# The first batch runs its sixteen feed-forward tiles in a row; the second batch is prepared like the later ones

## The chip, the cores and the metric

The kernel runs on one core of one Trainium2 chip. The metric is device time in microseconds, from launch to end. The profile describes one execution of it; its span runs from the first to the last instruction on the core.

## The reference

Two stages, in float32. The weights `moe_w_in` and `moe_w_out` arrive as 8-byte floats, which the kernel has to turn into 4-byte ones itself.

```python
B, H, S, Ns, D = (8, 8, 512, 32, 64)
scores  = scale * x @ state^T        ; a  = softmax(scores)  ; xread = a  @ state
scores2 = scale * state @ x^T        ; a2 = softmax(scores2) ; sread = a2 @ x
attn = concat([xread, sread], axis=2)               # per head: 512 + 32 rows of 64
x = attn.transpose(0, 2, 1, 3).reshape(8 * 544, 512)
h = x @ w_in                                        # 512 -> 2048
g = h * clip(h + 3, 0, 6) / 6
out = g @ w_out                                     # 2048 -> 512
```

## The kernel before

**Tiling.** The 2048 feed-forward columns are 16 tiles of 128, in 4 chunks of 4. A batch (512 tokens) meets the 16 tiles one by one; tile and batch together are a *step*, numbered n. Of a step, `first(n)` makes h for 512 tokens (6 matmuls 128x512: each factor is held as a high and a low part, and a product is three matmuls), ScalarE (ACT) and VectorE (DVE) make g from it and split it (`g_hi`, `g_lo`), and `second(n)` multiplies by one tile of `w_out` into the four accumulators `acc0` to `acc3` (12 matmuls), two steps later (`LAG`). Tile 0 of batch 0 is computed "plain", in float32 without the split. Step numbers 128 to 143 are the rows of `sread` of all batches together.

**W'.** `xread @ w_in` is not formed: `wprime` multiplies the batch's state with a chunk of `w_in` (lines L507, in `all_heads`), and `first` multiplies the softmax weights (`aT_hi`, `aT_lo`) with that product (`wp_hi`, `wp_lo`).

**Preparing a batch.** Scores, softmax over the states, softmax over the tokens, and `sread`. Batches from `TURNED` on are loaded in 32x32 blocks, so that DVE transposes alone turn x and state (`load_turned`, `load_state`: 16 loads of x into `raw` buffers; `attention`). Earlier batches are loaded plainly and turned by TensorE (PE) against an identity (`take_in`, lines L591 and L620, copied out by L624); their scores use `apart`, the state with heads set apart by zeros (`all_heads_apart`, L520). Batch 0 has a variant of its own (`tokens_by_rows`, L685 to L719). Before the change `TURNED` is 2. Batch 1's x is loaded into an output buffer `ot`, turned, and loaded again into `xb` later for `sread`.

**Weights.** 16 tiles each of `w_in` and `w_out` are fetched by the SP queue, in pairs (1 MB) into four staging buffers `early0` to `early3` or singly (0.5 MB) into the three `raw` buffers. A tile is decoded by ACT (L372, `tops`) and DVE (L377, join); a `w_out` tile is then split by ACT (L403) and DVE (L405). A staging buffer takes its next pair only when the one before is decoded (for `w_out`: split). `PLACES` says which pair goes where.

**Order.** Every operation is told to a planner (`Plan`) with a cost, a rank and its inputs; `Plan.order` lists them, and each engine runs its share in that order. The first operations are listed outright, by number, in the table `OPENING`; behind its end ranks decide. Where the plan has PE idle ahead of the first step, `issue` puts dummy matmuls (`wake`).

**Sequence of steps.** Weights arrive while steps run, so before the change the first two batches share them: tiles 0 to 3 of batch 0, 0 to 7 of batch 1, 4 to 15 of batch 0, 8 to 15 of batch 1. Each of the two batches then ends in two parts, added together in `ot`:

```python
segments = [(0, 0, 1), (1, 0, 2), (0, 1, NCH), (1, 2, NCH)]
segments += [(b, 0, NCH) for b in range(2, B + 1)]
```

Of the kernel before, what the change touches and what calls it, by code (L numbers as in the profile page):

```python
# [59 lines left out]
class Plan:  # L60
# [6 lines left out]
    WARM = 7.5  # L67
# [132 lines left out]
def tile_state_attention_then_hardswish_ffn(  # L200
# [82 lines left out]
    def Q(rank, size, do, reads=(), writes=(), after=()):  # L283
        return plan.add("Q", 0.45, rank, do, reads, writes, after, size)
# [131 lines left out]
    TURNED = 2  # L416
# [30 lines left out]
    def x_key(b):  # L447
        return ("ot", "x1") if b == 1 else ("xb", b)

    def read_key(b):  # L450
        return ("xb", b)

    def x_tile(b, read=False):

        if b == 1 and not read:
            t = get(x_key(b), lambda: outp.tile([P, J, DO], F32, name="ot")).rearrange("p j e -> p (j e)")
        else:
            t = get(read_key(b), lambda: att.tile([P, J, H, D], F32, name="xb", bufs=1))  # L460
            if b >= TURNED:
                return t.rearrange("p j h d -> p h j d")
            t = t.rearrange("p j h d -> p (j h d)")
        return t.rearrange("p (h j d) -> p h j d", h=H, j=J)

    def x_parts(b, read=False):
        key = read_key(b) if read else x_key(b)
# [44 lines left out]
    def all_heads_apart(b, out):  # L512
# [3 lines left out]
        for u in range(NG):  # L516
            for q in range(NQ):
                for i in range(2):
                    rows, cols = slice(i * D, (i + 1) * D), slice(u * S // 2, (u + 1) * S // 2)
                    nc.tensor.matmul(  # L520
                        out[i][q * NS : (q + 1) * NS, cols], apart[rows, b, q, u, i], xT(b, q)[rows, cols],
# [54 lines left out]
    def xT_key(b, q):  # L576
        return (("w_out_hi1", "w_in3")[b], "xT", q) if b < 2 else ("tmp", ("xT", b, q))

    def xT(b, q):

        if b == 0:
            return get(xT_key(0, q), lambda: cpool.tile(
                [P, NQ, S], F32, name="xT", tag="w_out_hi1"))[:, q]
        return w_in_of(3, "xT")[:, q] if b == 1 else tmp(xT_key(b, q))

    def take_in(b, rank, after=(), banks=None):
# [13 lines left out]
        for u in range(NG) if b < TURNED else ():  # L600
            for i in range(2):
                def put(u=u, i=i):
                    src = bank(st)[u * D : (u + 1) * D, :P].rearrange("p (q n) -> p q n", n=NS)
# [1 line left out]
                    copy(apart[i * D : (i + 1) * D, b, :, u, i], src)
# [279 lines left out]
    def put(c, ps, cols):  # L885
# [3 lines left out]
            [n for k, n in scores_at.items() if k in (0, ("L", 0), ("L", 1), ("C", 1))])  # L889

    def tokens_read(b, tag="ps_s"):
# [11 lines left out]
        def read():  # L903
            for u in range(NG):
                for j in range(J):
                    for q in range(NQ):
# [4 lines left out]
                            x_tile(b, True)[:, NG * q + u, j, :],  # L911
# [15 lines left out]
        return 1.0 + 0.11 * len(last), read, [*t_key, *x_parts(b, True), *last_key], [pr], then, first  # L927
# [28 lines left out]
    def first(n):  # L956
# [43 lines left out]
        rank = n if b < 2 else n - 1.5  # L1000
# [91 lines left out]
    segments = [(0, 0, 1), (1, 0, 2), (0, 1, NCH), (1, 2, NCH)]  # L1092
    segments += [(b, 0, NCH) for b in range(2, B + 1)]
# [94 lines left out]
    for b, s0 in (0, 4), (1, 8):  # L1188

        def late(b=b, s0=s0):  # L1190
            rank = lambda k: LATE[b] + k * LATE_STEP[b]
            states(b, rank, scores_by_columns(b, LATE[b] + 0.01, (), "L"))
            if b == 0:
                weights_turned(b, rank(7))
            else:
                load_x(1, AGAIN, (), True)
        at(LATE_TOLD[b], late)
    at(MOVED + 1, lambda: weights_moved(1, MOVED, [first_of[MOVED]]))
    fetch(2, 28, 20)
    for b in range(2, B):  # L1200
        s0 = {2: 24}.get(b, 16 * (b - 1))
        begin(b, s0, 4 if b == 3 else 0)
        if b < B - 1:
            fetch(b + 1, s0 + 9 + (4 if b == 3 else 0), s0 + 9 + (4 if b == 3 else 0))
# [76 lines left out]
```

## Time and profile before

| | us |
|---|---|
| runs of the kernel | 652.94, 654.09, 655.06 (median 654.09) |
| the profiled execution | 654.81 |
| its span | 652.7 |
| granted TensorE clock, mean | 1.000 |

The profile gives, by engine, busy time in the span and in stretches of it; a timeline of instructions with the idle time ahead of each and what ended it; the chain of work that ended last, followed back from the end; and the DMA issues with their time to landing. PE, PEld, DVE, ACT and SP are TensorE's matmuls, its weight loads, VectorE, ScalarE and the queue of SyncE that issues DMAs.

### The profile page before, as it was taken

The page shows a single profiled execution, that of the slowest core. Times are in us where ns is not written, and L with a number is a line of the kernel's source. Part 1 is how long each engine was busy: PE and PEld are TensorE (multiplying, and loading weights), DVE is VectorE, ACT ScalarE, POOL GpSimd, SP SyncE. Part 2 cuts the span into 40 slices and gives each one's busy share as a digit, 9 for nine tenths or more (in the row PEclk, how much of TensorE's full clock was granted, in tenths as well). Part 3 has the DMA queues.
Part 4 walks back from the last instruction along what each step waited for, and adds up shares of the span by engine and source line. Part 5 has one row for each costly group of instructions (what it writes and reads, how often), then busy time and mean ns, then how long its engine had stood idle before and what let it go on. Part 6 is the DMA issues. An engine that isn't in the chain of part 4 may idle for free.

```text
span 652.7 us, 10021 instructions
## 1 busy us (share of the span) xinstructions
PE 642.7 (98%) x3991; PEld 502.7 (77%) x3991; DVE 394.8 (60%) x687; ACT 299.1 (46%) x524; POOL 1.2 (0%) x7
## 2 busy tenths in 40 slices
PE   7899999999999999999999999999999999999997
PEld 6576777777877877787868787787778787788896
DVE  5997657568747756944586356834595344443552
ACT  5778577334434343633344344534344333433542
POOL 0000000000000000000000000000000000000000
PEclk9999999999999999999999999999999999999999
DMA  8851442514253054132131405041131001000101
GB/s 255 331 178 51 150 173 90 88 26 131 32 134 65 15 82 111 25 52 46 67 66 22 76 1 134 2 69 27 66 66 31 3 1 65 1 1 1 65 1 32
DMA packets 124399, 46.25 MB, mean 71 GB/s; under 512 B 111041, under 2 KB 118721, under 8 KB 124097
## 3 DMA queue, kind: packets, MB, share of 16 engines
q1 hardware_dynamic: 124208, 45.36, 27.3%
q8 instruction: 31, 0.51, 0.3%
q10 hardware_dynamic: 144, 0.26, 0.1%
q14 instruction: 16, 0.12, 0.1%
HBM read 33.02 MB, written 8.91 MB: 64 GB/s over the span
## 4 chain that ended last, share of the span: by engine, by line
PE 94%; DMA 3%; ACT 1%; SPq 1%; DVE 1%; issue 0%
PE acc L951 56%; PE ps_h L951 29%; PE ps_s L507 4%; PE ps_h L507 2%; DMA ot<-in_x_dram 1%; DMA early<-in_moe_w_out_dram 1%; PE ps_h L908 1%; PE acc L1020 1%; DMA st_raw<-in_state_dram 0%; ACT tops L372 0%; SPq L426 0%; PE ps_h L980 0%; PE ps_s L520 0%; SPq L476 0%; DVE w_in L377 0%
## 5 line engine op out<-in xcount | busy, mean ns | idle before, releaser
L951 PE MATMUL acc<-w_out_hi,g_hi 128*128 128x512 f32 x540 | 214.1, 396 | 0.0
L951 PE MATMUL acc<-w_out_lo,g_hi 128*128 128x512 f32 x540 | 210.8, 390 | 0.0
L951 PE MATMUL acc<-w_out_hi,g_lo 128*128 128x512 f32 x540 | 210.5, 390 | 0.0
L1001 ACT ACTIVATE g<-ps_h,three 128x512 f32<-128x512 f32 (+1 forms) x144 | 95.6, 665 | 210.7 <-PE ps_h L951 210.5
L1003 DVE SCALAR_TENSOR_TENSOR g<-g,ps_h 128x512 f32<-128x512 f32 (+1 forms) x144 | 94.7, 658 | 146.0 <-ACT g L1001 144.8
L951 PEld LDWEIGHTS acc<-w_out_hi,g_hi 128*128 128x128 f32 x540 | 101.5, 188 | 34.6 <-issue 12.4
L299 DVE TENSOR_TENSOR g_lo<-g,g_hi 128x512 fp32r<-128x512 f32 (+1 forms) x143 | 94.2, 659 | 54.8 <-ACT g_hi L298 53.3
L298 ACT CAST g_hi<-g 128x512 fp32r<-128x512 f32 (+1 forms) x143 | 85.2, 596 | 84.8 <-DVE g L1003 79.3
L951 PEld LDWEIGHTS acc<-w_out_hi,g_lo 128*128 128x128 f32 x540 | 101.5, 188 | 21.4
L951 PEld LDWEIGHTS acc<-w_out_lo,g_hi 128*128 128x128 f32 x540 | 101.6, 188 | 19.8 <-issue 0.3
L951 PE MATMUL ps_h<-aT_hi,wp_hi 128*128 128x512 f32 (+1 forms) x254 | 93.0, 366 | 0.2 <-ACT wp_hi L298 0.2
L951 PE MATMUL ps_h<-aT_hi,wp_lo 128*128 128x512 f32 (+1 forms) x254 | 92.4, 364 | 0.1
L951 PE MATMUL ps_h<-aT_lo,wp_hi 128*128 128x512 f32 (+1 forms) x254 | 92.2, 363 | 0.0
L951 PEld LDWEIGHTS ps_h<-aT_hi,wp_hi 128*128 128x128 f32 x254 | 47.9, 189 | 11.2 <-issue 1.2
L951 PEld LDWEIGHTS ps_h<-aT_hi,wp_lo 128*128 128x128 f32 x254 | 47.9, 189 | 8.0 <-DVE wp_lo L299 0.5
L951 PEld LDWEIGHTS ps_h<-aT_lo,wp_hi 128*128 128x128 f32 x254 | 48.0, 189 | 7.8
L951 PE MATMUL ps_h<-aT_hi,wp 128*128 128x512 f32 x128 | 44.6, 390 | 0.0
L951 PEld LDWEIGHTS ps_h<-aT_hi,wp 128*128 128x128 f32 x128 | 24.0, 188 | 5.0
L951 PE MATMUL ps_h<-aT_lo,wp 128*128 128x512 f32 x64 | 24.9, 390 | 0.0
L299 DVE TENSOR_TENSOR wp_lo<-ps_s,wp_hi 128x512 fp32r<-128x512 f32 (+1 forms) x36 | 20.9, 608 | 5.4 <-ACT wp_hi L298 5.4
L372 ACT CAST tops<-early 128x512 f16<-128x512 bf16 x25 | 19.1, 787 | 9.7 <-DMA early<-in_moe_w_in_dram 5.0
L507 PE MATMUL ps_s<-w_in,stT 64*32 64x512 f32 (+1 forms) x352 | 22.1, 553 | 0.1
(131 smaller groups left out, 433.4 us busy)
## 6 DMA issues: line engine op xcount, KB each, us to landing
xb<-in_x_dram SPq DMA_DIRECT2D x32, 256.0 KB, 4.3
out_dram<-ot SPq DMA_DIRECT2D x8, 1024.0 KB, 4.3
early<-in_moe_w_in_dram SPq DMA_DIRECT2D x7, 1023.0 KB, 8.0
raw<-in_x_dram SPq DMA_DIRECT2D x96, 64.0 KB, 2.1
early<-in_moe_w_out_dram SPq DMA_DIRECT2D x4, 1023.5 KB, 6.0
raw<-in_moe_w_out_dram SPq DMA_DIRECT2D x7, 511.8 KB, 6.1
raw<-raw SPq DMA_DIRECT2D x96, 32.0 KB, 2.0
ot<-in_x_dram SPq DMA_DIRECT2D x4, 256.0 KB, 6.8
```

The costliest lines, as they stand in the source:

```text
L298: S_(cost, rank, lambda: nc.scalar.copy(hi(), src()), reads, [writes[0]])
L299: V(cost, rank, lambda: nc.vector.tensor_tensor(lo(), src(), hi().bitcast(F32), op=ALU.subtract), [*reads, writes[0]], [writes[1]])
L372: nc.scalar.copy(out[..., 1], digits(pieces().bitcast(BF16), 2, i))
L507: nc.tensor.matmul(out[u][cols, :], made["stT", b][rows, cols], moving(q)[rows], start=True, stop=True,)
L908: nc.tensor.matmul(bank(pr)[cols, u * D : (u + 1) * D], e2T(b, u)[:, j * P + q * NS : j * P + (q + 1) * NS], x_tile(b, True)[:, NG * q + u ...
L951: nc.tensor.matmul(ps, l, r, start=start and k == 0, stop=stop and k == n - 1)
L1001: S_(cost + 0.05, rank, lambda: nc.scalar.activation(g(), bank(ps)[:, :width], AF.Relu, bias=three), [ps], [g_key])
L1003: V(cost, rank, lambda: nc.vector.scalar_tensor_tensor(g(), g(), 6.0, bank(ps)[:, :width], op0=ALU.min, op1=ALU.mult), [ps], [g_key])
L1020: nc.tensor.matmul(bank(acc), made["g_hi", n][:, js], plain_out[i][1](), start=opens, stop=closes)
```

## The change

`TURNED` becomes 1, and the segments are the batches in their order:

```diff
-    TURNED = 2
+    TURNED = 1
...
-    segments = [(0, 0, 1), (1, 0, 2), (0, 1, NCH), (1, 2, NCH)]
-    segments += [(b, 0, NCH) for b in range(2, B + 1)]
+    segments = [(b, 0, NCH) for b in range(B + 1)]
...
-    apart = sread_t.rearrange("p q m -> p (q m)").rearrange(
-        "p (b q u i n) -> p b q u i n", b=2, q=NQ, u=NG, n=NS)
-    nc.gpsimd.memset(apart[:, 0], 0.0)
+    apart = sread_t.rearrange("p q m -> p (q m)")[:, : 2 * NG * NQ * NS].rearrange(
+        "p (q u i n) -> p q u i n", q=NQ, u=NG, n=NS)
+    nc.gpsimd.memset(apart, 0.0)
...
-        return ("ot", ("wp", b, c)) if 1 < b < B and (NCH * b + c) % 3 == 2 else ("wp", (b, c))
+        return ("ot", ("wp", b, c)) if 0 < b < B and (NCH * b + c) % 3 == 2 else ("wp", (b, c))
...
-        return (("w_out_hi1", "w_in3")[b], "xT", q) if b < 2 else ("tmp", ("xT", b, q))
+        return ("w_in3", "xT", q) if b == 0 else ("tmp", ("xT", b, q))
...
-    for b, s0 in (0, 4), (1, 8):
-
-        def late(b=b, s0=s0):
-            rank = lambda k: LATE[b] + k * LATE_STEP[b]
-            states(b, rank, scores_by_columns(b, LATE[b] + 0.01, (), "L"))
-            if b == 0:
-                weights_turned(b, rank(7))
-            else:
-                load_x(1, AGAIN, (), True)
-        at(LATE_TOLD[b], late)
-    at(MOVED + 1, lambda: weights_moved(1, MOVED, [first_of[MOVED]]))
-    fetch(2, 28, 20)
-    for b in range(2, B):
-        s0 = {2: 24}.get(b, 16 * (b - 1))
-        begin(b, s0, 4 if b == 3 else 0)
+    def late():
+        rank = lambda k: LATE[0] + k * LATE_STEP[0]
+        states(0, rank, scores_by_columns(0, LATE[0] + 0.01, (), "L"))
+        weights_turned(0, rank(7))
+    at(LATE_TOLD, late)
+    fetch(1, 4, 4)
+    for b in range(1, B):
+        s0 = {1: 6}.get(b, 16 * (b - 1))
+        begin(b, s0)
...
-    load_state(1, RANKS["st1"])
...
-    load_x(1, RANKS["x1"])
...
-        if 1 < b < B and n % (2 * FPC) == 0:
+        if 0 < b < B and n % (2 * FPC) == 0:
...
-        if n == 0:
-            take_in(1, [*RANKS["take1"], RANKS["take1"][1]], [scores_at[0]])
-            rank1 = lambda k: RANKS["soft1"][k]
-            tokens_by_columns(1, rank1, scores_by_columns(1, RANKS["scores1"], [wp_at[0, 0, 2]]))
```

So batch 1's x and state come as 32x32 blocks during batch 0's steps, its x is loaded into `xb` once (the copy in `ot` is gone), and its W' is formed for two chunks at a time. The planner's costs for DMA issues rise a little (0.45 to 0.49, 0.9 to 1.35), its `WARM` falls from 7.5 to 4.5, and the ranks of the opening are written anew. `OPENING` is a new list, of some 660 numbers where there were some 490; both begin alike:

```diff
-5 2 1 4 0 3 24 6 80 28 81 36 30 32 27 33 31 29 40 37 79 93 34 41 78 50 35 38 25 85 51 66 52 39 26 42 53 11 67
+5 2 1 0 24 3 4 35 11 80 36 27 6 29 30 28 93 31 32 33 14 49 34 41 25 19 50 51 37 26 52 42 38 39 53 43 57 54 44
```

What the list does is seen on the engines. Lines of code move down or up a little: L620 of before is L617 of the change, L716 is L713, L377 is L384, L403 is L410, L405 is L412, L363 is L370.

PE, the stretch that ends in the first step of batch 0. L620 turns the last quarter of batch 1's x, L716 turns batch 0's finished softmax weights (`ot` is the buffer of either), L507 is W' of `w_in` tiles, L980 is `first(0)`. Before:

```order
L620 MATMUL ps_s<-ident,ot 128x128 x4
L716 MATMUL acc_302<-ident,ot 128x128 x4
L716 MATMUL acc_310<-ident,ot 128x128 x4
L507 MATMUL ps_s<-w_in_190,stT 32x256 x8
L980 MATMUL ps_h<-w_in_315,tmp 128x512 x2
L507 MATMUL acc_352<-w_in_190,stT 32x128
L507 MATMUL acc_353<-w_in_190,stT 32x128
```

The same place in the change (L520 are batch 0's scores over the tokens, the `wake` rows are dummies):

```order
L520 MATMUL ps_s<-w_in_132,sread_t 32x256 x16
L1235 LDWEIGHTS wake
L1235 MATMUL ps_h<-wake 128x256
L1235 LDWEIGHTS wake
L1235 MATMUL ps_h<-wake 128x256
L1235 LDWEIGHTS wake
L1235 MATMUL ps_h<-wake 128x256
L713 MATMUL acc_302<-ident,ot 128x128 x4
L713 MATMUL acc_308<-ident,ot 128x128 x4
```

No turn of batch 1's x stands ahead of L713 any more, W' of tiles 2 and 3 stands behind `first(0)` now, and batch 0's scores over the tokens have come ahead of it.

SP's queue, the weight loads behind those of the opening. Before:

```order
L363 DMA early_342<-in_moe_w_in_dram 128x4x1023
L363 DMA early_347<-in_moe_w_out_dram 128x2047
L363 DMA early_362<-in_moe_w_in_dram 128x4x1023
L363 DMA early_365<-in_moe_w_in_dram 128x4x1023
L363 DMA early_504<-in_moe_w_out_dram 128x2x2047
L363 DMA raw<-in_moe_w_out_dram 128x2047 x2
L363 DMA early_602<-in_moe_w_out_dram 128x2x2047
```

In the change, with the same sizes:

```order
L370 DMA early_390<-in_moe_w_in_dram 128x4x1023
L370 DMA raw<-in_moe_w_out_dram 128x2047
L370 DMA early_444<-in_moe_w_out_dram 128x2x2047
L370 DMA raw<-in_moe_w_out_dram 128x2047
L370 DMA early_497<-in_moe_w_out_dram 128x2x2047
L440 DMA st_raw<-in_state_dram 32x4x32 x4
L370 DMA raw<-in_moe_w_out_dram 128x2047
L370 DMA early_562<-in_moe_w_in_dram 128x4x1023
L370 DMA early_595<-in_moe_w_in_dram 128x4x1023
L370 DMA early_641<-in_moe_w_out_dram 128x2x2047
L370 DMA early_683<-in_moe_w_out_dram 128x2x2047
L494 DMA raw<-in_x_dram 32x16x32 x16
```

The pairs 444, 562 and 641 use one staging buffer (`early2`) one after the other, and 497, 595 and 683 another (`early3`); the 16 block loads of batch 1's x stand behind them, where none stood before.

DVE in the change, where these pairs are decoded among the steps (L1000 and `g_lo` belong to steps, `wp_lo` to W', `tops` rows are joins, `w_out_lo` splits):

```order
L412 TENSOR_TENSOR w_out_lo_545<-early_497,w_out_hi_534 128x1024
L306 TENSOR_TENSOR g_lo<-g,g_hi 128x512
L384 SCALAR_TENSOR_TENSOR raw<-raw,tops 128x512
L384 SCALAR_TENSOR_TENSOR w_in_613<-early_562,tops 128x4x128
L306 TENSOR_TENSOR g_lo<-g,g_hi 128x512
L384 SCALAR_TENSOR_TENSOR w_in_613<-early_562,tops 128x4x128
L306 TENSOR_TENSOR wp_lo<-ps_s,wp_hi 128x256
L1000 SCALAR_TENSOR_TENSOR g<-g,ps_h 128x512
L384 SCALAR_TENSOR_TENSOR raw<-raw,tops 128x512
L306 TENSOR_TENSOR wp_lo<-ps_s,wp_hi 128x256
L384 SCALAR_TENSOR_TENSOR w_in_613<-early_595,tops 128x4x128 x2
```

A join that waits for its pair holds up the `g_lo` rows queued behind it.

More of the change, by code (lines that the diff above doesn't have):

```diff
@@ L24 @@
 RANKS = {
-    "load": [-0.94, -21.67, -18.89, -39.86, 11.26, 12.58, 4.72],
-    "decode": [-40.16, 63.8, 0.9, -42.8, -3.86, -8.59, -1.85], "sooner": [-6.2, 2.14, 9.66, 2.27],
-    "out_sooner": -1.74, "late": [55.57, 156.43], "late_step": [-17.01, -157.0], "halves": [47.68, -16.73],
+    "load": [-40.0, -30.0, -18.0, -28.0, -17.0, -16.0, -15.0],
+    "decode": [-40.0, -30.0, -18.0, -28.0, -17.0, -16.0, -15.0], "sooner": [0, 4.0, 4.0, 4.0],
+    "out_sooner": -1.74, "late": [4.0], "late_step": [0.3], "halves": [47.68, -16.73],
     "out_halves": [17.05, 4.87, -12.12, -22.97], "halves_first": 5.19, "again": 77.67, "moved": 22,
@@ L66 @@
     AFTER = {"T": 0.25, "V": 0.12, "S": 0.12, "Q": 0.0}
-    WARM = 7.5
+    WARM = 4.5
     def __init__(self, slots, transfer):
@@ L283, in Q @@
     def Q(rank, size, do, reads=(), writes=(), after=()):
-        return plan.add("Q", 0.45, rank, do, reads, writes, after, size)
+        return plan.add("Q", 0.49, rank, do, reads, writes, after, size)
     def get(key, make):
@@ L436, in load_state @@
         if b < TURNED:
-            plan.add("Q", 0.9, rank, load, (), [key], after, 200.0)
+            plan.add("Q", 1.35, rank, load, (), [key], after, 400.0)
             return
@@ L447, in x_key, with x_tile, x_parts, load_x @@
     def x_key(b):
-        return ("ot", "x1") if b == 1 else ("xb", b)
-    def read_key(b):
         return ("xb", b)
-    def x_tile(b, read=False):
-        if b == 1 and not read:
-            t = get(x_key(b), lambda: outp.tile([P, J, DO], F32, name="ot")).rearrange("p j e -> p (j e)")
-        else:
[L460 to L467, printed above, removed]
+    def x_tile(b):
+        t = get(x_key(b), lambda: att.tile([P, J, H, D], F32, name="xb", bufs=1))
+        if b >= TURNED:
+            return t.rearrange("p j h d -> p h j d")
+        return t.rearrange("p j h d -> p (j h d)").rearrange("p (h j d) -> p h j d", h=H, j=J)
+    def x_parts(b):
+        key = x_key(b)
         return [(*key, "q", q) for q in range(NQ)] if b < TURNED else [(*key, j) for j in range(J)]
-    def load_x(b, rank, after=(), read=False):
-        for k, key in enumerate(x_parts(b, read)):
+    def load_x(b, rank, after=()):
+        for k, key in enumerate(x_parts(b)):
             def load(k=k):
@@ L475, in load @@
                     hs = slice(k * NG, (k + 1) * NG)
-                    nc.sync.dma_start(x_tile(b, read)[:, hs], x[b, hs].rearrange("h (p j) d -> p h j d", j=J))
+                    nc.sync.dma_start(x_tile(b)[:, hs], x[b, hs].rearrange("h (p j) d -> p h j d", j=J))
                 else:
-                    nc.sync.dma_start(x_tile(b, read)[:, :, k, :], x_v[b, k])
+                    nc.sync.dma_start(x_tile(b)[:, :, k, :], x_v[b, k])
             Q(rank[k] if isinstance(rank, list) else rank, 268.0 if b < TURNED else 417.0, load, writes=[key], after=after)
@@ L520, in all_heads_apart @@
                     nc.tensor.matmul(
-                        out[i][q * NS : (q + 1) * NS, cols], apart[rows, b, q, u, i], xT(b, q)[rows, cols],
+                        out[i][q * NS : (q + 1) * NS, cols], apart[rows, q, u, i], xT(b, q)[rows, cols],
                         start=True, stop=True,
@@ L576, in xT_key @@
     def xT_key(b, q):
-        return (("w_out_hi1", "w_in3")[b], "xT", q) if b < 2 else ("tmp", ("xT", b, q))
+        return ("w_in3", "xT", q) if b == 0 else ("tmp", ("xT", b, q))
     def xT(b, q):
-        if b == 0:
-            return get(xT_key(0, q), lambda: cpool.tile(
-                [P, NQ, S], F32, name="xT", tag="w_out_hi1"))[:, q]
-        return w_in_of(3, "xT")[:, q] if b == 1 else tmp(xT_key(b, q))
+        return w_in_of(3, "xT")[:, q] if b == 0 else tmp(xT_key(b, q))
     def take_in(b, rank, after=(), banks=None):
@@ L604, in put @@
                     copy = nc.vector.tensor_copy if u == i else nc.scalar.copy
-                    copy(apart[i * D : (i + 1) * D, b, :, u, i], src)
+                    copy(apart[i * D : (i + 1) * D, :, u, i], src)
                 (V if u == i else S_)(0.22, RANKS["apart"] if b == 0 else URGENT, put, [st], [("apart", b, u, i)])
@@ L686, in scores @@
                             out[:, k, u], xT(0, q)[:, (u * 2 + k) * P : (u * 2 + k + 1) * P],
-                            apart[:, 0, q, u].rearrange("p i n -> p (i n)"), start=True, stop=True,
+                            apart[:, q, u].rearrange("p i n -> p (i n)"), start=True, stop=True,
                         )
@@ L733, in scores_by_columns @@
         ps = [("ps_s", (name, b, u)) for u in range(NG)]
-        riders = [tokens_read(b - 1, "ps_h")] if b >= TURNED or name == "L" and b else []
+        riders = [tokens_read(b - 1, "ps_h")] if b >= TURNED else []
         def run():
@@ L888, in put @@
             bank(ps)[:, cols].rearrange("p (q n) -> p q n", n=NS)), [ps], [("sread", c)],
-            [n for k, n in scores_at.items() if k in (0, ("L", 0), ("L", 1), ("C", 1))])
+            [n for k, n in scores_at.items() if k in (0, ("L", 0))])
     def tokens_read(b, tag="ps_s"):
@@ L910, in read @@
                             e2T(b, u)[:, j * P + q * NS : j * P + (q + 1) * NS],
-                            x_tile(b, True)[:, NG * q + u, j, :],
+                            x_tile(b)[:, NG * q + u, j, :],
                             start=(j == 0),
@@ L926, in first @@
                 nc.tensor.transpose(bank(pr)[:, place(1)], tmp(key)[:, : NG * D], ident)
-        return 1.0 + 0.11 * len(last), read, [*t_key, *x_parts(b, True), *last_key], [pr], then, first
+        return 1.0 + 0.11 * len(last), read, [*t_key, *x_parts(b), *last_key], [pr], then, first
     def tokens_read_alone(b, rank, after=()):
@@ L998, in first @@
         cost = 0.1 + 0.53 * width / S
-        rank = n if b < 2 else n - 1.5
+        rank = n if b < 1 else n - 1.5
         S_(cost + 0.05, rank, lambda: nc.scalar.activation(
@@ L1113, in tile_state_attention_then_hardswish_ffn @@
     SOONER = RANKS["sooner"]
-    LATE_TOLD, AGAIN, MOVED = (8, 12), RANKS["again"], RANKS["moved"]
+    LATE_TOLD = 3
     LATE, LATE_STEP = RANKS["late"], RANKS["late_step"]
@@ L1179, in fetch @@
     def fetch(b, step, turned):
-        s0 = 12 if b == TURNED else step - 7
+        s0 = 0 if b == TURNED else step - 7
         at(s0 + 1, lambda: load_state(b, s0, [first_of[s0]]))
@@ L1187, in tile_state_attention_then_hardswish_ffn @@
     at(PLAIN if PLAIN < FPC else 9, halves_of_first, RANKS["halves_first"])
[L1188 to L1202 removed]
+    def late():
[7 more added lines that the diff above has]
+        begin(b, s0)
         if b < B - 1:
[L1204 removed]
+            fetch(b + 1, s0 + 9 + (4 if b == 1 else 0), s0 + 9 + (4 if b == 1 else 0))
     s = NF * (B - 1) + 3
@@ L1225, in tile_state_attention_then_hardswish_ffn @@
         k, c = n // FPC, i // FPC
-        if 1 < b < B and n % (2 * FPC) == 0:
+        if 0 < b < B and n % (2 * FPC) == 0:
             wprime(b, [(c, 0, FPC), (c + 1, 0, FPC)], n - 2.6, None, [first_of[n - 3]])
             plan.ops[first_of[n - 2]][4].add(wp_at[b, c, 0])
-        elif b < 2 and n % FPC == 0:
+        elif b < 1 and n % FPC == 0:
             ends = wp_parts[b, c][1:] + [FPC]
```

39 rows, old and new, of tables (OPENING, RANKS) are left out of this document.

## The prediction

> **What bounds the kernel now.** I read the busy times first, then the same by stretches, then the timeline of PE up to its first step.
>
> ```profile
> PE 642.7 (98%) x3991; PEld 502.7 (77%) x3991; DVE 394.8 (60%) x687; ACT 299.1 (46%) x524; POOL 1.2 (0%) x7
> 0.00:20.00 20.00, 14.94 (x122) 12.05 (x123) 11.29 (x37) 11.35 (x23) 1.17 (x7) 1.00 0.85 277
> 20.00:40.00 20.00, 19.94 (x143) 12.33 (x142) 19.75 (x37) 15.95 (x31) 0.00 (x0) 1.00 0.70 251
> 40.00:60.00 20.00, 20.00 (x141) 14.79 (x141) 15.62 (x29) 15.84 (x34) 0.00 (x0) 1.00 0.39 137
> 80.00:100.00 20.00, 19.77 (x190) 14.95 (x188) 11.28 (x22) 14.08 (x29) 0.00 (x0) 1.00 0.46 158
> 160.00:232.00 72.00, 72.00 (x458) 54.92 (x457) 48.32 (x83) 29.70 (x51) 0.00 (x0) 1.00 0.29 59
> ```
>
> The columns behind the stretch are its length, then busy time of PE, PEld, DVE, ACT and POOL, the granted clock, DMA's share and GB/s. From 20 us on PE has no idle time worth a microsecond and its clock is whole: the kernel ends at the start of its first step plus PE's work. Two things can move its end, the opening and PE's list. A third is seen in 20 to 40 us: DVE is busy 19.75 of 20, so there the opening's other work (decoding weights, batch 1's softmax) is as close to the limit as PE.
>
> ```profile
> 15.57 1.81 PE L1250 MATMUL ps_h<-wake 128*128 128x256 bf16 x15
> 19.03 0.63 PE L620 MATMUL ps_s<-ident,ot 128*128 128x128 f32 x4 [1.65 <-DMA ot<-in_x_dram]
> 19.50 1.04 PE L716 MATMUL acc<-ident,ot 128*128 128x128 f32 x8
> 20.59 0.90 PE L507 MATMUL ps_s<-w_in,stT 64*32 64x256 f32 x16
> 21.42 1.99 PE L980 MATMUL ps_h<-w_in,tmp 128*128 128x512 f32 x4
> 23.33 0.45 PE L507 MATMUL acc<-w_in,stT 64*32 64x128 f32 x16
> 23.57 1.07 PE L520 MATMUL ps_s<-w_in,sread_t 64*32 64x256 f32 x32
> 24.57 0.50 PE L951 MATMUL ps_h<-aT_hi,wp_hi 128*128 128x512 f32 x1
> 17.18 1.05 DVE L708 TENSOR_TENSOR ot<-ot,s 128x256 f32<-128x256 f32 x3
> 10.26 8.64 DMA ot<-in_x_dram
> ```
>
> Columns: start, time, engine, line, in brackets the idle time ahead and what ended it; the last row is one of the chain that ended last. Step 0 starts at 21.42. It needs L716, the turn of batch 0's softmax weights, which DVE finished at 17.18 + 1.05 = 18.23. But in PE's queue the last quarter of batch 1's x stands ahead, whose transfer ended at 18.9. So PE waits for a batch that isn't due yet.
>
> **The change, term by term.** The sum is made against the profiled execution, 654.81 us (span 652.7 and 2.1 around it); the median of the runs shown is 0.72 less.
>
> *The opening.* With batch 1's x out of PE's queue, L716 could start at 18.23 instead of 19.50: 1.27 gained. W' of tiles 2 and 3 goes behind step 0: 20.59 to 21.42 is 0.83, of which part was waiting for the copies of L716's result anyway. Also, 1 MB of x leaves the head of the DMA queue, at the 277 GB/s of the first stretch about 3.7 us of transfers, so weights land sooner. These waited for weights:
>
> ```profile
> 9.89 0.77 ACT L372 CAST tops<-early 128x512 f16<-128x512 bf16 x1 [1.57 <-DMA early<-in_moe_w_in_dram]
> 18.31 1.41 ACT L372 CAST tops<-early 128x512 f16<-128x512 bf16 x2 [1.39 <-DMA early<-in_moe_w_in_dram]
> 5.54 0.28 DVE L605 COPY sread_t<-ps_s 64x128 f32<-64x128 f32 x1 [3.33 <-PE ps_s L591]
> 10.69 0.69 DVE L377 SCALAR_TENSOR_TENSOR w_in<-early,tops 128x512 uint32<-128x512 uint32 x1 [1.27 <-ACT tops L372]
> 19.10 1.34 DVE L377 SCALAR_TENSOR_TENSOR w_in<-early,tops 128x512 uint32<-128x512 uint32 x2 [0.88 <-ACT tops L372]
> 31.43 0.68 DVE L299 TENSOR_TENSOR g_lo<-g,g_hi 128x512 fp32r<-128x512 f32 x1
> 40.73 1.27 DVE L299 TENSOR_TENSOR aT_lo<-tmp,aT_hi 128x512 fp32r<-128x512 f32 x2
> ```
>
> Against it, DVE's queue now has two more joins ahead of the end of the softmax (2 x 0.60), and three copies of batch 1's state fewer. The change to the opening is worth between 0 (DVE's added rows eat it) and 1.27 + 0.83 + 0.7 of the softmax's own waits = 2.8. I take **-2.0**, nearer the upper end, since the wait that goes is the one that ended last.
>
> *DVE as the second bound.* Two 128x512 rows take 1.27 together where one takes 0.68, so one costs 0.60 in a row. Up to the first `g_lo`, which `second(1)` needs, the change has 25 rows of that class (15.2), 16 of 128x256 (0.33 each, 5.3) and 20 small ones (3.0): 23.5. Before it is 22.2, and that row ended at 32.0, so DVE had idled 9.8. If the 1.27 and 0.88 above go, it idles 7.6, and the row ends at 31.1. PE gets there, from step 0 at 19.4, after `first` 0 to 3 (2.0 and 3 x 1.36), four plain products of 0.95, two W' of 0.6 and three turnarounds of 0.3: 12, at 31.4. The two meet; nothing is lost there, and nothing is spare.
>
> *PE's list behind step 0.* Before, three score blocks of L520 stand there (one above, 23.57 to 24.57, two more like the next row), in the change one of L507's form:
>
> ```profile
> 41.28 1.09 PE L520 MATMUL ps_s<-xT,sread_t 64*32 64x256 f32 x32
> 42.30 0.50 PE L951 MATMUL ps_h<-aT_hi,wp_hi 128*128 128x512 f32 x1
> 63.91 1.09 PE L507 MATMUL ps_s<-w_in,stT 64*32 64x512 f32 x16
> 64.93 0.50 PE L951 MATMUL ps_h<-aT_hi,wp_hi 128*128 128x512 f32 x1
> 160.36 1.09 PE L507 MATMUL ps_s<-w_in,stT 64*32 64x512 f32 x16
> 161.24 1.06 PE L507 MATMUL ps_h<-w_in,stT 64*32 64x512 f32 x16
> 162.23 0.50 PE L951 MATMUL acc<-w_out_hi,g_hi 128*128 128x512 f32 x1
> 54.08 0.66 PE L507 MATMUL ps_s<-w_in,stT 64*32 64x256 f32 x16
> 54.67 0.50 PE L951 MATMUL acc<-w_out_hi,g_hi 128*128 128x512 f32 x1
> 169.16 0.39 PE L951 MATMUL ps_h<-aT_hi,wp 128*128 128x512 f32 x1
> ```
>
> To the next instruction each block of L520 takes 1.02, so 2 x 1.02 = 2.04 go. W' of batch 1 was three chunks of 1.02 and one in halves of 0.59, 4.24; two pairs of 162.23 - 160.36 = 1.87 take its place, 3.74: 0.5 less. Batch 0 has one chunk in halves that was whole, 0.16 more, the W' of tile 1 (0.24) moves ahead of step 0, and the 0.83 taken out of the opening comes back as 0.6. Sum -2.04 - 0.5 + 0.16 - 0.24 + 0.6 = **-2.0**. Steps, read-outs and turns are as many as before, and from batch 2 on (169.16) the list is the same.
>
> *The staging loop.* All 16 tiles are due within batch 0's 16 steps, not 28. In `early2` three pairs follow each other, each loaded only when the pair before is decoded, and DVE's joins wait in line ahead of `g_lo` rows.
>
> ```profile
> DMA to landing us min/median/max: 4.9/7.0/12.6
> early<-in_moe_w_in_dram SPq DMA_DIRECT2D x7, 1023.0 KB, 8.0
> 112.41 9.27 SPq L494 DMA_DIRECT2D raw<-in_x_dram  x16
> raw<-in_x_dram SPq DMA_DIRECT2D x96, 64.0 KB, 2.1
> ```
>
> Adding DVE's rows up from 31.1 with a landing of 4.9, the joins of 562 and 641 wait 1.2 and 0.6, and `g_lo` of step 8 or so ends at 62.4, 1.9 ahead of PE. Each further microsecond of landing counts three times, less that 1.9. With 8.0, the median of `w_in` pairs, it is 3 x 3.1 - 1.9 = 7.4 lost; with less than 5.5, nothing. The long landings of before belong to the opening, where several pairs were issued together; in the change pairs 444 to 683 are mostly two in flight. I take 1.0, and keep 0 and 7.4.
>
> *Batch 1's preparation.* Its 16 loads wait for a `raw` buffer, which DVE's splits free at about 61. They take 9.27 + 2.1 = 11.4, so x lands at 72.4; the scores stand in PE's queue at about 73.8. From there DVE has 30 rows to `aT_lo`, which end near 91, when PE has no more of batch 0 but one step. I take 0.5; if either slips, batch 1 waits as long, up to 3.
>
> This load comes in pieces of 128 bytes, and the Trainium skill speaks against such a load (DMA: Bandwidth & Descriptors, section "Specifications": below 512 bytes a transfer does not reach line rate). By that rule the load would stretch where it shares the engines with weights. In the row above SP issued a piece every 0.58 us, with little beside it; no run here shows it beside weights.
>
> **Sum.** -2.0 - 2.0 + 1.0 + 0.5 = -2.5, so 652.3 for an execution like the profiled one, and **651.6** beside the median of 654.09.
>
> **The rivals.**
> - *DVE keeps the opening.* For it speaks the 19.75 of 20, and that DVE's list to the first `g_lo` is 1.3 longer. Then step 0 comes early and `second(1)` waits till 23.5 + 9.8 = 33.3: the opening's 2.0 are gone, and 654.09 - 0.5 = 653.6, no change.
> - *Landings of 7.0*, the median of all pairs: 3 x 2.1 - 1.9 = 4.4 instead of 1.0, with the rest as forecast 655.0, no change. Against it: DMA is 0.39 busy between 40 and 60 us.
> - *The staging loop binds*: slower. At 8.0 it is 7.4 instead of 1.0: 658.0. It decides from about 7.3 on (3 x 2.4 - 1.9 = 5.3, which makes 655.9). Its place is the joins of 562 and 641, and the share of DVE's idle time there.
> - *The 128-byte load is stretched* by sharing the engines: taking twice the 11.4, x lands at 83.8, 10 later than PE's scores, and 654.09 - 2.5 + 10 = 661.6. Against it: only one weight load stands behind it in SP's queue. The Trainium skill's page named above is what speaks for it.
> - *The opening gains in full and no loop waits*: -2.8 - 2.0 = -4.8, 649.3.
>
> **Chances.** A measurement of this kernel can tell 0.3% (1.96 us) from no change, so faster is below 652.13 and slower above 656.05. Forecast 0.42 (650.0 to 653.0, two thirds of it faster); full gain 0.24; DVE keeps the opening 0.12; landings of 7.0 0.10; loop binds 0.09; stretched load 0.03. That makes faster 0.42 x 0.66 + 0.24 = 0.52, slower 0.12, and the rest, 0.36, within. The range from 648.8 to 656.5 leaves out the two slow cases and the ends of the others.
>
> **What would show it.** PE's L977 (step 0) near 19.4, with no idle time of a DMA of x ahead of L713. `second(1)` near 31. Idle time of PE between 30 and 95 us below 2; if there is more, its releaser tells which: DVE `g_lo` behind a join that waited for `early` (loop), DVE `aT_lo` (batch 1). Batch 2's first step near 166.5 instead of 169.16. I am wrong if step 0 comes no earlier than 21, or if a wait on `early` pairs holds PE for more than 3.

## The result and the profile after

The changed kernel takes **657.28 us** (median of 20 runs, 654.80 to 662.38), the kernel before 653.75 (20 runs, 652.92 to 655.97). The ratio is 1.0054, with an interval from 1.0039 to 1.0070: slower by 0.54%. The forecast was 651.6, and its range ended at 656.5. The profiled execution of the changed kernel is one of the quicker ones, 655.46 with a span of 653.7, so two things have to be explained: 1.0 us that the two spans show, and some 2 us more between this execution and the median, which no single profile shows.

Busy time of the whole span and of the stretches, with the same columns as before; one stretch is new, 120 to 140 us, and the last row is that stretch of the kernel before:

```profile
PE 641.6 (98%) x3934; PEld 500.3 (77%) x3934; DVE 393.0 (60%) x685; ACT 293.1 (45%) x510; POOL 1.2 (0%) x7
20.00:40.00 20.00, 19.63 (x112) 11.85 (x111) 18.28 (x37) 17.36 (x38) 0.00 (x0) 1.00 0.92 322
40.00:60.00 20.00, 19.57 (x125) 13.46 (x124) 16.55 (x27) 17.76 (x31) 0.00 (x0) 1.00 0.75 248
80.00:100.00 20.00, 20.00 (x112) 15.21 (x111) 17.61 (x35) 11.32 (x21) 0.00 (x0) 1.00 0.10 21
120.00:140.00 20.00, 17.08 (x147) 13.02 (x145) 10.05 (x16) 5.10 (x8) 0.00 (x0) 1.00 0.47 86
120.00:140.00 20.00, 20.00 (x100) 15.43 (x98) 10.91 (x17) 5.91 (x10) 0.00 (x0) 1.00 0.24 39
```

Where the forecast looked for waits, from 20 to 100 us, PE loses 0.37 and 0.43 by these rows (a third wait there, of 1.0, is hidden in a busy row and is shown further down). Where it did not look, between 120 and 140 us, PE stands idle for 2.9 us; the kernel before was busy for the whole of that stretch. The steps themselves, start and time, from PE's timeline:

```profile
17.63 1.09 PE L713 MATMUL acc<-ident,ot 128*128 128x128 f32 x8 [0.56 <-DVE ot L705]
19.54 1.88 PE L977 MATMUL ps_h<-w_in,tmp 128*128 128x512 f32 x4
31.62 0.39 PE L948 MATMUL acc<-w_out_hi,g_hi 128*128 128x512 f32 x1
169.49 0.39 PE L948 MATMUL ps_h<-aT_hi,wp 128*128 128x512 f32 x1
```

Step 0 starts at 19.54 (before 21.42), `second(1)` at 31.62, and batch 2's first step at 169.49, where it was 169.16 before and 166.5 was forecast. So the opening's gain is there at 32 us and gone at 169. The timeline of all engines around the idle stretch, in order of start, tells why:

```profile
131.98 0.60 SPq L494 DMA_DIRECT2D raw<-in_x_dram  x1
132.35 0.39 PE L948 MATMUL acc<-w_out_hi,g_lo 128*128 128x512 f32 x1
132.91 0.71 DVE L607 STREAM_TRANSPOSE tmp<-raw 128x512 f32<-128x512 f32 x1 [2.74 <-DMA raw<-in_x_dram]
134.23 0.71 DVE L607 STREAM_TRANSPOSE tmp<-raw 128x512 f32<-128x512 f32 x1 [0.61 <-DMA raw<-in_x_dram]
134.86 0.65 DVE L306 TENSOR_TENSOR wp_lo<-ps_h,wp_hi 128x512 fp32r<-128x512 f32 x1
135.44 0.67 DVE L306 TENSOR_TENSOR g_lo<-g,g_hi 128x512 fp32r<-128x512 f32 x1
135.66 0.47 PE L948 MATMUL ps_h<-aT_hi,wp_hi 128*128 128x512 f32 x1 [2.92 <-DVE wp_lo L306]
```

Read it from below. PE's `first` at 135.66 needs one of the two `ps_h` banks (the places that its products go to), which `wp_lo` still reads. DVE has been idle for 2.74 us by then; `wp_lo` could have run, but in DVE's queue two transposes of batch 2's x (L607) stand ahead of it, and these wait for block loads, the last of which SP issues only at 131.98. PE's step of 0.23 from one matmul to the next became 135.66 - 132.35 = 3.31 here: **3.1 us lost**.

SP is late because its queue mixes two jobs. The first of these rows are of the changed kernel, piece by piece; the last one is of the kernel before, where all 16 loads of batch 2 had been issued by 121.7 and the first transpose ran at 130.66:

```profile
116.70 0.59 SPq L879 DMA_DIRECT2D raw<-raw  x1
117.33 0.60 SPq L494 DMA_DIRECT2D raw<-in_x_dram  x1
117.98 0.59 SPq L879 DMA_DIRECT2D raw<-raw  x1
```

```profile
130.66 0.70 DVE L610 STREAM_TRANSPOSE tmp<-raw 128x512 f32<-128x512 f32 x1
```

L879 are the moves of batch 1's softmax weights (e2) into the form that `sread` needs. The kernel before issued its moves behind all the loads; the new `OPENING` has the 16 moves and the 16 loads alternate, one issue each 0.64 us.

For the other 2 us there are the granted clocks of the 20 runs. Six runs have a mean clock of 0.999 or 1.000 and take 654.80 to 656.68; fourteen have 0.997 or less and take 656.87 to 662.38. The two longest (661.78 and 662.38, clock 0.987 and 0.986) lose some 5 us more than the median; no profile shows where.

### The profile page after: what moved, and what is told of

It is laid out like the page before. It is cut to its first block, busy times and chain, and to the rows that moved or that the text cites. A ratio compares the mean times of both kernels' runs of the same rounds, so it can differ in the third digit from the quotient of the medians.

```text
span 653.7 us, 9891 instructions
## 1 busy us (share of the span) xinstructions
PE 641.6 (98%) x3934; PEld 500.3 (77%) x3934; DVE 393.0 (60%) x685; ACT 293.1 (45%) x510; POOL 1.2 (0%) x7
## 4 chain that ended last, share of the span: by engine, by line
PE 85%; SPq 4%; DMA 4%; DVE 3%; ACT 2%; issue 1%; DVEq 0%; ACTq 0%
PE acc L948 51%; PE ps_h L948 27%; PE ps_s L507 4%; PE ps_h L507 2%; SPq L879 1%; SPq L494 1%; DMA raw<-in_x_dram 1%; DMA early<-in_moe_w_out_dram 1%; PE ps_h L905 1%; SPq L478 1%; ACT tops L379 1%; DMA early<-in_moe_w_in_dram 1%; DMA raw<-raw 1%; DVE w_in L384 0%; ACT g L998 0%
## 5 line engine op out<-in xcount | busy, mean ns | idle before, releaser
L1000 DVE SCALAR_TENSOR_TENSOR g<-g,ps_h 128x512 f32<-128x512 f32 (+1 forms) x144 | 94.3, 657 | 150.7 <-ACT g L998 149.9
L948 PEld LDWEIGHTS acc<-w_out_lo,g_hi 128*128 128x128 f32 x540 | 101.5, 188 | 19.6
L948 PE MATMUL ps_h<-aT_hi,wp_hi 128*128 128x512 f32 (+1 forms) x246 | 90.4, 367 | 3.3 <-DVE wp_lo L306 2.9
L948 PE MATMUL ps_h<-aT_hi,wp_lo 128*128 128x512 f32 (+1 forms) x246 | 89.1, 362 | 0.4 <-DVE wp_lo L306 0.4
L948 PE MATMUL ps_h<-aT_lo,wp_hi 128*128 128x512 f32 (+1 forms) x246 | 89.1, 362 | 0.0
L948 PEld LDWEIGHTS ps_h<-aT_hi,wp_hi 128*128 128x128 f32 x246 | 46.4, 189 | 13.4 <-issue 3.6
L948 PEld LDWEIGHTS ps_h<-aT_lo,wp_hi 128*128 128x128 f32 x246 | 46.4, 189 | 8.2 <-DVE aT_lo L306 0.5
L948 PE MATMUL ps_h<-aT_hi,wp 128*128 128x512 f32 x144 | 50.2, 389 | 0.0
L948 PEld LDWEIGHTS ps_h<-aT_hi,wp 128*128 128x128 f32 x144 | 27.0, 188 | 5.7
L607 DVE STREAM_TRANSPOSE tmp<-raw 128x512 f32<-128x512 f32 x28 | 19.1, 699 | 15.9 <-DMA raw<-in_x_dram 12.3
L948 PE MATMUL ps_h<-aT_lo,wp 128*128 128x512 f32 x72 | 28.0, 389 | 0.0
L507 PE MATMUL ps_s<-w_in,stT 64*32 64x512 f32 (+1 forms) x320 | 19.6, 548 | 0.0
```

The costliest lines, as they stand in the source:

```text
L507: nc.tensor.matmul(out[u][cols, :], made["stT", b][rows, cols], moving(q)[rows], start=True, stop=True,)
L607: V(0.7, rank[0], lambda q=q, key=key: nc.vector.transpose(xT(b, q), made[key][:, q % 2]), [(*key, q % 2, u, k) for u in range(2) for k in ...
L948: nc.tensor.matmul(ps, l, r, start=start and k == 0, stop=stop and k == n - 1)
L1000: V(cost, rank, lambda: nc.vector.scalar_tensor_tensor(g(), g(), 6.0, bank(ps)[:, :width], op0=ALU.min, op1=ALU.mult), [ps], [g_key])
```

## The experiments

**Two theories.** Theory 1: the wait in DVE's queue is the whole loss; it costs 3.1 us by itself, and such an idle stretch of PE also costs the granted clock in most runs. Theory 2: the clock is lost elsewhere, for instance in the new opening, and comes back by no edit at 132 us.

**The changed kernel again** (`c0`, no edit), beside the variants on one chip.

> The changed kernel as it is, on the chip that the other runs of this set use. Both theories expect what was measured for it: a median near 657, some 3 us above the kernel before, the profiled gap of TensorE at 132 us, and times that go with the granted clock: about 655.4 at 0.999 to 1.000, about 657.5 at 0.995 to 0.997. If the spread with the clock is a thing of one chip, it shows here.

Measured: 657.80 (655.90 to 660.37, 6 runs), ratio to before 1.0052, interval 1.0034 to 1.0069. Five of six runs are at 0.997 or less, one at 0.999 (655.90). The profiled execution is the slowest of them, and this time the trace shows the clock go. PE's rows around the idle stretch, and below them the stretches with PE's busy time and the granted clock (behind the 0.00 of POOL):

```profile
135.22 0.39 PE L948 MATMUL acc<-w_out_hi,g_lo 128*128 128x512 f32 x1
138.66 0.47 PE L948 MATMUL ps_h<-aT_hi,wp_hi 128*128 128x512 f32 x1 [3.05 <-DVE wp_lo L306]
138.96 0.40 PE L948 MATMUL ps_h<-aT_lo,wp_hi 128*128 128x512 f32 x1
139.19 0.39 PE L948 MATMUL ps_h<-aT_hi,wp_lo 128*128 128x512 f32 x1
139.73 0.63 PE L948 MATMUL ps_h<-aT_lo,wp_hi 128*128 128x512 f32 x1
140.16 0.63 PE L948 MATMUL ps_h<-aT_hi,wp_lo 128*128 128x512 f32 x1
138.00:142.00 4.00, 3.34 (x10) 2.42 (x10) 1.82 (x4) 1.30 (x2) 0.00 (x0) 0.69 0.01 2
142.00:146.00 4.00, 4.00 (x88) 2.35 (x87) 2.44 (x5) 0.00 (x0) 0.00 (x0) 0.88 0.02 4
146.00:150.00 4.00, 4.00 (x20) 3.30 (x19) 3.97 (x10) 2.37 (x5) 0.00 (x0) 1.00 0.00 0
```

After 3.05 us of idle time, and three matmuls later, the distance from one start to the next goes from 0.23 (138.96 to 139.19) to 0.43 (139.73 to 140.16). The loss is 4 x 0.31 + 4 x 0.12 = 1.7 us, or 3.4 us at half rate. This drop is not all by which the execution is longer: its span is 4.8 above that of the profile shown first, and 2.9 of them are lost ahead of the idle stretch (its last product before it starts at 135.22, not 132.35), 2.1 of these in the opening. The profile shown first has the idle stretch (2.92) and no drop. The Trainium skill (TensorE: Matmul & The Clock Gate, section "Why this matters for your kernels") asks for no idle gaps of PE over about 3 us, and here the trace agrees; its section "Part 1: The HAM clock gate" puts the idle window at about 3.4 us, and here 3.05 was enough.

**The wait taken out of DVE's queue** (`e1`). In `OPENING`, 521 and 520 are the two transposes, 577 is `wp_lo`, 568 the `g_lo` behind it:

```diff
-607 521 567 600 520 577 606 601 568 639 602 603 617 640 524 641 604 608 526 547 618 550 615 548 525 549 610
+607 567 600 577 606 601 568 521 520 639 602 603 617 640 524 641 604 608 526 547 618 550 615 548 525 549 610
```

> The changed kernel with one edit in VectorE's order: the two transposes of batch 2's x that wait for the last block loads (L607) stand behind the next wp_lo and g_lo, not ahead of them. TensorE's gap before the first product at 132.35 (3.1 us) should go; the scores of batch 2, two groups later, still want the second transpose (ends near 134.9), so 0.3 to 0.5 us of stall stay there. Span about 2.7 us below the changed kernel's profiled 653.7, so near 651. Theory 1 (the gap itself costs the granted clock in most runs): clocks go back to 0.999 or 1.000 in nearly all runs, median 652 to 653, some 4 to 5 us below the changed kernel and 1 us below the kernel before. Theory 2 (the clock is lost for another reason, the opening for instance): clocks stay near 0.997 and the median is near 654.5, 2.7 us below the changed kernel.

Measured: 653.67 (652.94 to 654.05, 11 runs), ratio to before 0.9985, interval 0.9977 to 0.9994; span 651.2; the clock 0.998 to 1.000 in all 11 runs. That is 4.1 below the changed kernel on the same chip, where theory 2 had 2.7. What stays of the wait has moved to the scores of batch 2 and is 0.84, more than the 0.3 to 0.5 expected, since the turn that leads the scores takes the `ps_h` bank of a `g` row, which now stands behind the transposes:

```profile
132.17 0.71 DVE L607 STREAM_TRANSPOSE tmp<-raw 128x512 f32<-128x512 f32 x1 [1.48 <-DMA raw<-in_x_dram]
133.43 0.71 DVE L607 STREAM_TRANSPOSE tmp<-raw 128x512 f32<-128x512 f32 x1 [0.54 <-DMA raw<-in_x_dram]
134.06 0.65 DVE L1000 SCALAR_TENSOR_TENSOR g<-g,ps_h 128x512 f32<-128x512 f32 x1
134.76 0.33 PE L923 MATMUL ps_h<-ident,tmp 128*128 128x128 f32 x1 [0.84 <-DVE g L1000]
```

**The loads put together in SP's queue** (`e2`), with DVE's order as it is in the changed kernel. SP's rows from 122.5 us on, of the changed kernel (-) and the variant (+):

```diff
-L494 DMA raw<-in_x_dram 32x16x32
-L879 DMA raw<-raw 32x8x32 x3
-L494 DMA raw<-in_x_dram 32x16x32 x2
-L879 DMA raw<-raw 32x8x32
-L494 DMA raw<-in_x_dram 32x16x32 x2
-L879 DMA raw<-raw 32x8x32 x2
-L494 DMA raw<-in_x_dram 32x16x32
-L879 DMA raw<-raw 32x8x32
-L494 DMA raw<-in_x_dram 32x16x32
-L879 DMA raw<-raw 32x8x32 x7
+L494 DMA raw<-in_x_dram 32x16x32 x7
+L879 DMA raw<-raw 32x8x32 x14
```

> The changed kernel with one edit in SyncE's order, VectorE's as it is: in the places between 122.5 and 132 us the eight loads of the last half of batch 2's x are issued first and the seven e2 moves of batch 1 behind them, where the changed kernel mixes them. If the 3.1 us come from the last load standing behind those moves (issued 131.98, TensorE waiting from 132.35), the last load goes out near 128, both transposes run by 131.6 and the gap goes: span 650.5 to 651, the scores then waiting at most 0.5 us for the last move. If the loads are late for a reason other than their place in the queue (landing of 1 to 2 us grown by contention), the gap stays above 1.5 us. For the clock the same two theories as with the edit of VectorE's order: clock 0.999 to 1.000 and median near 652.5, or clock near 0.997 and median near 654.5.

Measured: **652.97** (652.55 to 653.70, 11 runs), ratio to before 0.9979, interval 0.9970 to 0.9989, clock 0.998 to 1.000 in all runs. The variant is quicker than both kernels. SP's queue, DVE's and PE's stretch now read:

```profile
123.67 4.07 SPq L494 DMA_DIRECT2D raw<-in_x_dram  x7
127.78 4.51 SPq L879 DMA_DIRECT2D raw<-raw  x7
130.07 1.30 DVE L607 STREAM_TRANSPOSE tmp<-raw 128x512 f32<-128x512 f32 x2
131.29 0.65 DVE L306 TENSOR_TENSOR wp_lo<-ps_h,wp_hi 128x512 fp32r<-128x512 f32 x1
120.00:140.00 20.00, 20.00 (x160) 15.70 (x159) 13.10 (x24) 5.88 (x10) 0.00 (x0) 1.00 0.53 86
166.17 0.39 PE L948 MATMUL ps_h<-aT_hi,wp 128*128 128x512 f32 x1
```

The last load goes out at 127.7 instead of 131.98, both transposes run without a wait, PE has no idle time in the stretch, and batch 2's first step starts at 166.17. So the loads were late by their place in SP's queue, not by a slow landing, and either end of the chain, DVE's order or SP's, undoes the loss.

**The wait kept, PE kept busy in it** (`e3`). One more entry in `OPENING` ahead of the product that waits; its 22 products fill a bank that nobody reads:

```diff
+    T(0.0, 1.0e6, lambda: [nc.tensor.matmul(bank(("ps_s", "spare"))[:, :256], wake[:, :P], wake, start=True, stop=True) for _ in range(22)], [], [("ps_s", "spare")])
```

> The changed kernel with its gap kept, but TensorE kept busy in it: 22 more products of the kernel's wake tile (128x256, 0.12 us each, about 2.7 us), whose result nobody reads, ahead of the product that waits at 132.35. Nothing else waits for them, so the profiled span should stay near 653.7 (653.4 to 654.2). Theory 1 (the gap of 3 us costs the granted clock): clocks 0.999 to 1.000 in nearly all runs and median 655 to 655.7, 2 us below the changed kernel. Theory 2 (the clock is lost elsewhere): clocks stay at 0.995 to 0.999 and the median at 657.

Measured: 655.52 (654.68 to 656.64, 11 runs), ratio to before 1.0014, interval 1.0005 to 1.0023, clock 0.998 to 1.000 in all runs. The row of the wait is the same but for the idle time, 0.72 instead of 2.92:

```profile
132.79 2.58 PE L1234 MATMUL ps_s<-wake 128*128 128x256 bf16 x22
136.09 0.47 PE L948 MATMUL ps_h<-aT_hi,wp_hi 128*128 128x512 f32 x1 [0.72 <-DVE wp_lo L306]
```

PE gets through the useful work no earlier, and still the median is 657.80 - 655.52 = **2.3 us** lower than without the filling. Theory 2 falls: nothing in the opening was touched. The 4.8 us between the changed kernel and `e2` are so 2.3 of clock and 655.52 - 652.97 = 2.55 of the wait itself.

**A shorter and a longer idle stretch** (`e5` and `e6`, on another chip). `e5` is `e3` with `range(8)`. `e6` puts a memset on DVE ahead of `wp_lo`:

```diff
+    V(0.0, 1.0e6, lambda: nc.vector.memset(bank(("ps_s", "spare")), 0.0), [], [("ps_s", "spare")])
```

> The changed kernel with its gap at 132 filled by 8 of the wake products (1.0 us) instead of 22, so that TensorE idles about 2.1 us in one piece, not 3.1. If any idle stretch of a few microseconds costs the clock in proportion, the median lies about two thirds of the way from 655.5 (filled) to 657.8 (not filled), near 657.0, with half of the runs at 0.997. If it takes an idle stretch near 3 us or more, 2.1 us costs nothing: clocks 0.998 to 1.000 and a median of 655.2 to 655.8, like the fill of 2.7 us.

> The changed kernel with the gap made longer: one more instruction of VectorE (a memset of 128x512 in PSUM that nothing reads, 0.3 to 0.7 us) ahead of the wp_lo that TensorE waits for, so the gap grows from 3.1 to 3.4 to 3.8 us. If the clock is lost when the idle stretch passes a length near 3 us, now all runs lose it: clocks at 0.997 or less in every run, and the median rises by the added 0.3 to 0.7 plus 0 to 0.8, to 658.3 to 659.3. If the loss of 2 us does not hang on the length of the gap, the median rises by the added time alone, to 658.1 to 658.5, and some runs stay at 0.999 to 1.000 and near 656.2.

Measured for `e5`: 655.75 (655.31 to 657.39, 6 runs), ratio to before 1.0033, interval 1.0020 to 1.0045. Five runs are at 0.999 or 1.000 and take 655.31 to 655.93; one is at 0.997 and takes 657.39. Measured for `e6`: 659.26 (657.76 to 659.80, 5 runs), ratio to before 1.0078, interval 1.0064 to 1.0091. Four of five are at 0.993 to 0.997, and one kept 0.999 (657.76), so "every run" was too much. Its trace shows the drop as well:

```profile
135.36 0.48 DVE L1234 MEMSET ps_s<- 128x512 f32 x1
136.57 0.77 PE L948 MATMUL ps_h<-aT_hi,wp_hi 128*128 128x512 f32 x1 [3.74 <-DVE wp_lo L306]
138.00:146.00 8.00, 8.00 (x98) 5.02 (x97) 3.52 (x8) 1.55 (x4) 0.00 (x0) 0.73 0.01 3
```

If a mean clock of 0.997 or less is taken as the sign of the drop, it came in 0 of 11 runs at 0.7 us of idle time, 1 of 6 at 2.0, 5 of 6 (and 14 of 20) at 3, and 4 of 5 at 3.7. So it is rare at 2 us or less and frequent at 3 or more; finer steps than that are not shown by so few runs, and the lengths are those of the profiled executions. By the ratios, which allow for the two chips, `e5` lies 0.0019 above `e3`, with intervals that overlap a little; that a stretch of 2 us is free of cost is not shown.

**The kernel before, a second profile** (`b0`).

> The kernel before, unchanged, once more with a profile, to have a second row for the start of its first feed-forward product. In the first profile that was 21.42 us, in those of the changed kernel and its variants 19.0 to 19.6 with TensorE's matrix products at full rate from 5 us on, and 21.63 in the one profile where they ran at half rate until 15 us. If the opening gain of 2 us is real, 21 to 22 here at full rate; if it was a late start of that one profile, 19.5 to 20.5.

Measured: 655.66 in a single run, clock 0.995, step 0 at 22.35. It is not at full rate, so it does not answer the question as put; it shows something else, that the old opening could lose the clock too:

```profile
12.89 1.09 PE L620 MATMUL ps_s<-ident,ot 128*128 128x128 f32 x4 [1.63 <-DVE ot L699]
10.00:15.00 5.00, 3.37 (x23) 3.26 (x21) 3.02 (x8) 3.62 (x7) 0.00 (x0) 0.75 1.05 359
15.00:20.00 5.00, 5.00 (x40) 3.75 (x40) 4.28 (x19) 3.48 (x8) 0.00 (x0) 0.56 1.05 376
22.35 1.98 PE L980 MATMUL ps_h<-w_in,tmp 128*128 128x512 f32 x4
```

In the 39 runs of the kernel before that stood beside these variants the clock lay between 0.993 and 1.000; in the 33 of `e1`, `e2` and `e3` it was 0.998 or more. This matters for the ratios: on the chip of `e2`, the 12 runs of the kernel before at 0.998 or more have a median of 654.10, the 17 at 0.997 or less 654.96. For the opening itself the rows at full rate stand at 21.42 (one profile of before) against 19.54, 19.22, 19.03, 19.61, 18.98 and 19.29 (the changed kernel and its variants `e1`, `e2`, `e3`, `e5`, `e6`); `c0`, whose opening ran slow, has 21.63.

## Why the prediction was wrong

- **The opening, -2.0: right.** 21.42 became 19.54, and 19.0 to 19.6 in the variants. The wait on x is gone; L713 now waits 0.56 for the softmax.
- **DVE as the second bound: right.** `second(1)` was put at 31.4 by PE's list and starts at 31.62, without a wait.
- **The staging loop, +1.0: right in kind, half the size.** PE idles 0.40 at 44.82, and its step of 0.23 becomes 0.79 there, so 0.56 is lost. It happens earlier than forecast: DVE's `g` stood behind the join of a `w_out` pair that was issued at 34.65. The joins of the later pairs kept DVE waiting up to 1.3 us and left PE no idle time. The pairs of `w_in` land in a median of 5.8 where they took 8.0, as expected with two in flight.

```profile
42.83 1.34 DVE L384 SCALAR_TENSOR_TENSOR early<-early,tops 128x512 uint32<-128x512 uint32 x2 [0.53 <-ACT tops L379]
44.82 0.50 PE L948 MATMUL ps_h<-aT_hi,wp_hi 128*128 128x512 f32 x1 [0.40 <-DVE g L1000]
early<-in_moe_w_in_dram SPq DMA_DIRECT2D x7, 1023.0 KB, 5.8
```

- **Batch 1's preparation, +0.5: right in kind, twice the size.** Its loads start at 65.0, not 61. When the scores' turn comes in PE's queue, the last transpose of x still waits for its load:

```profile
65.04 8.29 SPq L494 DMA_DIRECT2D raw<-in_x_dram  x16
76.16 2.12 PE L507 MATMUL ps_s<-tmp,stT 64*32 64x512 f32 x16
76.45 0.71 DVE L607 STREAM_TRANSPOSE tmp<-raw 128x512 f32<-128x512 f32 x1 [1.55 <-DMA raw<-in_x_dram]
```

The row of 16 score products takes 2.12, where such a block takes 1.09 (the row at 63.91 in the prediction), so 1.0 us is lost inside a row that counts as busy. In `e2` it is 0.9. The loads were issued at 0.52 us a piece, with no weights beside them: the pairs ahead of them had been decoded by 61.4, and the next weight load was issued at 73.4. So no run here shows what the rule of the Trainium skill (DMA: Bandwidth & Descriptors, section "Specifications") would make of such a load beside weights.

- **PE's list, -2.0: right, as far as the sum shows it.** From step 0 to batch 2's first step the forecast has 166.5 - 19.4 = 147.1, with 1.0 + 0.5 of waits in it. In `e2`, without the stall, it is 166.17 - 19.03 = 147.14, with 0.6 and 0.9 lost in the same two places; in the changed kernel 149.95. That the two missed sizes make up for each other is luck, and so is an agreement to 0.04: PE's wait of 0.37 for `wp_lo` at 22.37 stood in no term.
- **The step that failed** is the sentence that closes the list: "from batch 2 on (169.16) the list is the same". It is true of PE's list, and it passed over how batch 2 is prepared, which happens inside batch 1's steps, ahead of 169.16. The prediction even quoted the row of those 16 loads (112.41, 9.27), but only as a price for batch 1's loads; it did not ask what stands between them in the new order, nor what waits behind their transposes in DVE's queue. That term was 0 and measured 2.55 to 3.1.
- **A second term was missing**: a lost clock. The first profile had a granted clock of 1.00 throughout, and the sum carried it over. It measured 2.3 in the median.
- Together: the forecast of 651.6, plus 3.1 and 2.3, is 657.0, and 657.28 was measured; it comes this near in part because smaller misses cancel. Of the rivals none came true; all the waits that they priced lay between 18 and 95 us. The test that had been named, batch 2's first step near 166.5, did tell the difference (169.49).

With the stall undone, the gain is 0.21% (`e2`, by the ratio) where 0.38% had been forecast. Even of this a part is clock that the kernel before loses: against its runs at 0.998 or more, `e2` gains 654.10 - 652.97 = 1.1 us. The profiled spans, 652.7 and 650.7, show what is missing. Batch 2's first step comes 3.0 earlier (169.16 to 166.17), but 0.8 of that goes in batch 2's own steps: batch 3's first step comes 2.2 earlier, 241.04 to 238.88. Most of it is one place, where PE's step of 0.23 becomes 0.90: PE idles for an output row of batch 1, which stands in DVE's queue behind transposes of batch 3's x, the same kind of wait in small:

```profile
173.31 0.71 DVE L607 STREAM_TRANSPOSE tmp<-raw 128x512 f32<-128x512 f32 x1 [1.22 <-DMA raw<-in_x_dram]
177.04 0.50 PE L948 MATMUL acc<-w_out_hi,g_hi 128*128 128x512 f32 x1 [0.52 <-DVE ot L1044]
```

That this wait goes with another order of DVE's rows was not tried.

## What to carry to other kernels

When a stage moves, follow the preparation of the *next* stage through every queue that it now shares: a stage whose own list is unchanged can still be starved by what has come to stand between its transfers. In an in-order queue, look for the instruction that may wait for a transfer and ask what the bottleneck needs from behind it; here moving two rows back by a few places was worth 4.1 us. Look for lost time in busy rows too: a row of several products that takes longer than its like elsewhere can hide a wait. And count an idle stretch of TensorE for more than its length: here one near 3 us cost 2.55 us by itself and another 2.3 in the median through the clock. Where the wait stayed, filling it with products that nobody reads won the 2.3 back.

## What the runs showed of the hardware

- One idle stretch of 3.05 us halved TensorE's rate for some 3.4 us; one of 2.92 us, in another execution of the same program, did not. The old opening dropped to half rate after less than that: in the second profile of before PE waited 1.63 us at 12.89, among sparse work, and the clock read 0.75 and 0.56 in the next two stretches. Length alone does not decide it.
- The granted clock in the records may miss a slow start. In the profile of `c0` it reads 1.00 from 0 to 15 us, yet its products take 0.22 us each where those of `e2` take 0.13 (first row `c0`, second row `e2`), and step 0 starts at 21.63 instead of 19.03. Three dummies ahead of them, which wait for nothing, are slower alike (0.84 us instead of 0.49), so that it is the clock is likely, but not shown:

```profile
7.83 3.51 PE L682 MATMUL ps_s<-sread_t,w_in 128*128 128x64 f32 x16
```

```profile
7.20 1.55 PE L682 MATMUL ps_s<-sread_t,w_in 128*128 128x64 f32 x12 [0.29 <-DVE sread_t L602]
```

- An issue on SP's queue took 0.58 us for a load of x in a row of loads (4.07 / 7), 0.64 for a move in a row of moves (4.51 / 7), and 0.64 where the two alternate. So the mixing itself cost a load at most 0.06; the order made the lateness.
